# Odd rows of u reversed in DRAM and loaded apart, in a linear-attention and S4 kernel whose order is a written list

## The chip, the cores and the metric

The kernel runs on one core of one Trainium2 chip. The metric is the device time of one execution in microseconds (us). The kernel before takes 230.46 us, the median of three runs (230.1, 230.46 and 230.79).

The core has five engines with a queue of instructions each: TensorE (PE in the profile; its weight loads are shown as PEld), VectorE (DVE), ScalarE (ACT), GpSimd (POOL) and SyncE (SP). Here SP only starts DMA transfers; ACT starts some, too. A queue is worked off in order: an instruction that waits holds up what stands behind it.

## The reference

Two independent halves are computed and put side by side in the output (2048 rows, 448 + 448 columns).

```python
# half A: linear attention with a softmax feature map (16 heads of 28)
qkv = (x @ wqkv)...
pq = einsum("bhsd,hdf->bhsf", q, w_phi);  pk = einsum("bhsd,hdf->bhsf", k, w_phi)
phi = concatenate([softmax(p), softmax(-p)])      # for q and for k
kv = einsum("bhsf,bhsd->bhfd", phi_k, v);  z = einsum("bhsf->bhf", phi_k)
a = (phi_q @ kv) / (phi_q . z + 1e-6), heads joined, @ wo
# half B: S4 convolution, D = 448 channels, N = 256 states, L = 2048
P = exp(dt * A * l)                               # complex, l = 0 .. L-1
K = einsum("dn,dnl,dn->dl", C, P, dt * B).real
y = irfft2(rfft2(K padded) * rfft2(u padded))[:L] + u * Dskip
return concatenate([a, y])
```

The change touches half B: how u comes in, and how one table of powers is made.

## The kernel before, in words

**Order.** The program doesn't issue an instruction when its line is reached. Each line adds an operation to a list (`Prog.add`), in program order, and at the end `prog.run(ORDER)` issues them in the order of a list of numbers written into the source. `ORDER` thus sets the order on every engine's queue. Three more lists go with it: `PLACES` gives each buffer its byte offset in one large SBUF tile (`sb`), so that buffers share bytes when their uses lie apart, `SLOTS` gives each PSUM product its banks, and `PICKS` says for each copy whether ACT or DVE makes it ("A", "V") and for each DMA whether SP or ACT starts it ("S", "Q"). The framework adds the waits: for data, and for bytes or banks that an earlier operation still uses.

**Half B.** The convolution goes through a transform of length 1024 for each of two blocks of u. `signal_spectrum(b)` makes u's spectrum. It needs, for each block, the even rows of u and the odd rows in reverse order, their sum `ab[:, 0]` and their difference `ab[:, 1]`; then 16 groups of products with the cosine tables `G1[0]` and `G1[1]` (512 KB each), whose results go to DRAM (`SUd`). Before, `load_u` brings pairs of rows (an even and the next odd row, 1792 bytes together) with two transfers of 64 partitions a block, and the odd rows are turned round on PE: four products with an anti-identity matrix, `REV`, and two copies out of PSUM to a buffer `ur`.

The kernel K is made from powers of exp(dt A). For the exponents 128, 16, 8, 32 and 64, ACT makes an exponential, a cosine and a sine, and DVE multiplies them (`PW`, each product 128 x 1792). The 256th powers come from squaring the 128th: `s2` are squares, `q256` takes the real part (`sub`) and the imaginary part (`stt`) in f32, and a copy writes it to `PW[256]` as bf16 with the two halves of each group of 56 columns interleaved. `TM`, `CB` are products of the coefficients with the 8th powers. Then, four times for a quarter of the channels (`tables(qt)`), DVE builds tables `U_` and `W` of powers, PE multiplies them (`build_k`), the result passes through DRAM (`scatter_k`) and PE transforms it (`kernel_spectrum`). `conv(qt)` multiplies the spectra on DVE and transforms back on PE (`inverse`).

**Half A** (`key_side`, `query_side`) is interleaved with this by `ORDER`.

**Line numbers.** Helpers record most operations: L186 is any DVE tensor-tensor operation (`tt`), L198 the DVE operation with a scalar and two tensors (`stt`), L206 an ACT function (`af`), L214 a copy, L217 a scaled copy, L229 PE products (`mms`), L239 PE transposes, L245 a transposing DMA, L249 a plain DMA.

Of the kernel before, what the change touches and what calls it, by code (L numbers as in the profile page):

```python
# [9 lines left out]
BF16 = mybir.dt.bfloat16  # L10
# [41 lines left out]
def _dft_tables():  # L52
# [24 lines left out]
    pid = np.zeros((128, 6, 128))  # L77
    for i, p in enumerate(ODD + [-1]):
        pid[np.arange(128), i, np.arange(128)] = p
    pid[np.arange(128), 5, 127 - np.arange(128)] = 1.0  # L80
# [49 lines left out]
def kernel(  # L130
# [22 lines left out]
    SUd = dram.tile([4, 128, 8, D_MODEL], BF16, name="SUd")  # L153
    KTd = dram.tile([4, 3, 128, D_MODEL], BF16, name="KTd")
# [36 lines left out]
    def add(o, a, b):  # L191
        tt(o, a, b, ALU.add)

    def sub(o, a, b):
        tt(o, a, b, ALU.subtract)
# [51 lines left out]
    def dma(eng, o, i):  # L247
        e = {"S": nc.sync, "Q": nc.scalar}[prog.queue()]
        prog.add("S", lambda: e.dma_start(out=o, in_=i))  # L249

    PID = sb([128, 6, 128])
# [3 lines left out]
    REV = PID[:, 5, :]  # L255
# [16 lines left out]
    def row_pairs(row, a):  # L272
        rs = u2.ap[0][0]
        return bass.AP(tensor=u2.tensor, offset=u2[row + 128 * (1 - a), 0].offset,
                       ap=[[2 * rs, 64], [256 * rs, 4], [1, 2 * D_MODEL]])

    ua = [sb([128, 4, 2, D_MODEL]) for _ in range(2)]

    def load_u(b):
        for a in range(2):  # L280
            dma("S", ua[b][64 * a:64 * a + 64].rearrange("p t r d -> p t (r d)"), row_pairs(1024 * b, a))

    eye = sb([112, 112])
# [75 lines left out]
    q128, q256 = (sb([128, 2, NCOL], F32) for _ in range(2))  # L359
# [24 lines left out]
    sub(q256[:, 0, :], s2[:, 0, :], s2[:, 1, :])  # L384
    stt(q256[:, 1, :], q128[:, 0, :], -2.0, q128[:, 1, :], ALU.mult, ALU.mult)
    copy(view(PW[256][:, 0, 0:1], [56, 32], [1, 2], [2, 28]), view(q256[:, 0, 0:1], [56, 32], [28, 2], [1, 28]))
# [32 lines left out]
    def signal_spectrum(b):  # L419
        ab = sb([128, 2, 4, D_MODEL])  # L420
        ur = sb([128, 4, D_MODEL])
        for tp in range(2):
            bs = prog.banks(2)
            mms([(psum[:, bs[k], 0:D_MODEL], REV, ua[b][:, 3 - 2 * tp - k, 1, :], dict(start=True, stop=True))
                 for k in range(2)])
            copy(ur[:, 2 * tp:2 * tp + 2, :], two(bs))
        add(ab[:, 0], ua[b][:, :, 0, :], ur)
        sub(ab[:, 1], ua[b][:, :, 0, :], ur)
# [459 lines left out]
).split()]  # L888
PLACES = [64 * int(i) for i in (
# [52 lines left out]
```

## Time and profile before

| | us |
|---|---|
| median of three runs | 230.46 |
| the profiled execution | 230.0 |
| its span, first to last instruction | 228.1 |
| DVE busy | 211.7 |
| PE busy | 201.5 |
| ACT busy | 194.5 |
| POOL busy | 8.9 |

The span's 40 slices are 5.7 us each; the digits in them are tenths of a slice. A "form" is an operation with its shapes. In a group of instructions "busy" is the time covered and the mean is that of one instruction, from its start to its end; neighbours on an engine overlap by some 0.1 us, so a run of them takes a little less than their sum. For DMAs, KB is the size of one transfer, and the time is from issue to landing. [...]

### The profile page before, as it was taken

What the parts mean: (1) busy time and instruction counts of PE and PEld (TensorE: products, weight loads), DVE (VectorE), ACT (ScalarE), POOL (GpSimd) and SP (SyncE); (2) the same over time, 40 slices, a digit from 0 to 9 for tenths busy, and PEclk for the clock granted to TensorE, in tenths of its full rate; (3) what the DMA queues carried; (4) which work ended last, traced back from release to release, by engine and by line L of the source; (5) the groups of instructions that cost most, each with busy time, mean ns of one, the idle gap of its engine ahead of it and who ended that gap; (6) DMA issues with size and microseconds to landing.
All of it is one profiled execution on the core that took longest, in us unless ns stands there. A gap on an engine that the chain in (4) does not pass through costs nothing.

```text
span 228.1 us, 7325 instructions
## 1 busy us (share of the span) xinstructions
PE 201.5 (88%) x3136; PEld 145.8 (64%) x3136; DVE 211.7 (93%) x268; ACT 194.5 (85%) x354; POOL 8.9 (4%) x26
## 2 busy tenths in 40 slices
PE   1155699999999999999795999999999998999994
PEld 1053346555558555897573878645677875799994
DVE  1899999999999999999999999999999994999990
ACT  3999999999999999999999999999798866454431
POOL 4000000200000200020000000100000000000000
PEclk9999889999999999999999999999999999999999
DMA  5969911548569959987757426053999149664163
GB/s 158 231 150 271 284 29 35 119 165 210 134 161 161 189 101 251 99 218 188 238 77 199 85 67 203 3 68 56 263 288 178 23 101 177 94 122 75 40 168 80
DMA packets 78247, 32.87 MB, mean 144 GB/s; under 512 B 64856, under 2 KB 76168, under 8 KB 77960
## 3 DMA queue, kind: packets, MB, share of 16 engines
q1 hardware_dynamic: 73080, 29.99, 60.8%
q10 hardware_dynamic: 5136, 2.43, 4.1%
q8 instruction: 24, 0.39, 0.7%
q14 instruction: 7, 0.06, 0.1%
HBM read 15.84 MB, written 8.49 MB: 107 GB/s over the span
## 4 chain that ended last, share of the span: by engine, by line
PE 53%; ACT 23%; DVE 16%; issue 5%; DMA 1%; DVEq 0%; ACTq 0%
PE psum L229 52%; DVE sbuf L186 14%; ACT sbuf L206 13%; ACT sbuf L214 9%; DVE sbuf L214 2%; DMA sbuf<-in_B_log_dt_dram 1%; ACT L206 1%; PE psum L239 1%; DVE sbuf L217 1%; DVE sbuf L198 0%; DVEq L186 0%; ACTq L206 0%; DVEq L214 0%; DVE sbuf L309 0%
## 5 line engine op out<-in xcount | busy, mean ns | idle before, releaser
L229 PE MATMUL psum<-sbuf 128*128 128x112 bf16 (+10 forms) x3088 | 199.3, 257 | 22.6 <-ACT sbuf L214 8.8
L186 DVE TENSOR_TENSOR sbuf<-sbuf 128x896 bf16<-128x896 bf16 (+11 forms) x214 | 190.6, 946 | 5.8 <-ACT sbuf L206 4.3
L229 PEld LDWEIGHTS <-sbuf 128*128 128x128 bf16 (+5 forms) x3088 | 143.3, 112 | 77.4 <-issue 23.9
L214 ACT CAST sbuf<-psum 128x448 bf16<-128x448 f32 (+8 forms) x124 | 80.1, 700 | 21.7 <-PE psum L229 19.0
L206 ACT ACTIVATE sbuf<-psum 128x512 bf16<-128x512 f32 (+6 forms) x154 | 83.5, 631 | 1.8 <-PE psum L229 1.0
L206 ACT ACTIVATE sbuf<-sbuf 128x896 bf16<-128x896 bf16 (+3 forms) x29 | 18.9, 684 | 2.4 <-DMA sbuf<-in_B_log_dt_dram 1.2
L214 DVE CAST sbuf<-psum 128x448 bf16<-128x448 f32 (+4 forms) x21 | 12.2, 596 | 7.0 <-PE psum L229 6.5
L206 ACT ACTIVATE sbuf<-psum,sbuf 128x896 f32<-128x896 f32 (+3 forms) x17 | 14.0, 827 | 0.5 <-ACT sbuf L214 0.5
L224 POOL MEMSET sbuf<- 128x224 bf16 (+7 forms) x21 | 8.4, 429 | 152.3 <-PE psum L229 67.3
L214 ACT COPY sbuf<-psum 112x896 bf16<-112x896 bf16 (+2 forms) x12 | 7.2, 638 | 2.1 <-PE psum L239 1.9
L203 ACT ACT_TABLE_LOAD x5 | 6.4, 1283 | 1.3 <-PEq L926 1.3
L206 ACT ACT_TABLE_LOAD x4 | 5.1, 1283 | 0.1
L214 DVE COPY sbuf<-sbuf 128x448 bf16<-128x448 bf16 (+2 forms) x13 | 4.2, 327 | 0.0
L239 PE MATMUL psum<-sbuf 112*112 112x112 bf16 (+1 forms) x48 | 3.4, 216 | 0.9 <-DVE sbuf L186 0.9
L239 PEld LDWEIGHTS <-sbuf 112*112 112x112 bf16 (+1 forms) x48 | 2.9, 120 | 1.5 <-DVE sbuf L186 1.0
L186 DVE TENSOR_TENSOR sbuf<-psum,sbuf 128x448 bf16<-128x448 f32 (+1 forms) x6 | 2.8, 489 | 0.0
L214 DVE CAST sbuf<-sbuf 128x1792 bf16<-128x1792 f32 (+1 forms) x4 | 2.8, 688 | 0.0
L217 DVE TENSOR_SCALAR sbuf<-sbuf 128x1568 bf16<-128x1568 bf16 x4 | 2.5, 617 | 0.0
L214 ACT COPY sbuf<-sbuf 128x224 bf16<-128x224 bf16 (+1 forms) x5 | 2.2, 444 | 0.0
L220 ACT ACTIVATE sbuf<-sbuf 128x1792 f32<-128x1792 f32 x1 | 1.8, 1785 | 0.0
L217 ACT ACTIVATE sbuf<-sbuf 112x448 bf16<-112x448 bf16 x1 | 0.6, 576 | 0.8 <-DVE sbuf L309 0.8
L198 DVE SCALAR_TENSOR_TENSOR sbuf<-sbuf,psum 128x128 f32<-128x128 f32 x4 | 1.1, 282 | 0.0
(8 smaller groups left out, 2.5 us busy)
## 6 DMA issues: line engine op xcount, KB each, us to landing
SUd<-sbuf SPq DMA_DIRECT2D x8, 448.0 KB, 3.6
sbuf<-SUd SPq DMA_DIRECT2D x4, 896.0 KB, 5.0
sbuf<-const SPq DMA_DIRECT2D x8, 384.0 KB, 4.2
sbuf<-in_B_u_dram SPq DMA_DIRECT2D x4, 448.0 KB, 6.3
out_dram<-sbuf SPq DMA_DIRECT2D x13, 112.0 KB, 2.8
out_dram<-sbuf SPq DMA_DIRECT2D x3, 448.0 KB, 3.5
sbuf<-const SPq DMA_DIRECT2D x2, 512.0 KB
sbuf<-const ACTq DMA_DIRECT2D x1, 1024.0 KB
```

The lines of the kernel that those rows point to most:

```text
L186: prog.add("V", lambda: nc.vector.tensor_tensor(out=o, in0=a, in1=b, op=op))
L198: prog.add("V", lambda: nc.vector.scalar_tensor_tensor(out=o, in0=a, scalar=s, in1=b, op0=op0, op1=op1))
L203: nc.scalar.preload_act_table_set("natural_log_exp_and_others")
L206: nc.scalar.activation(o, a, fn, **kw)
L214: either(lambda: nc.scalar.copy(o, a), lambda: nc.vector.tensor_copy(o, a))
L217: either(lambda: nc.scalar.activation(o, a, ACT.Copy, scale=s), lambda: nc.vector.tensor_scalar_mul(o, a, s))
L220: either(lambda: nc.scalar.activation(o, a, ACT.Square), lambda: nc.vector.tensor_tensor(out=o, in0=a, in1=a, op=ALU.mult))
L224: prog.add("G", lambda: nc.gpsimd.memset(o, v))
L229: nc.tensor.matmul(o, lhsT=l, rhs=r, **kw)
L239: nc.tensor.transpose(o, i, idn)
```

## The change

The source is changed in three places, and the four lists are written anew.

1. u. `reverse_u(b)` copies the odd rows of a block, last row first, from u in DRAM to a new DRAM tile `URd[b]` (4 x 128 rows of 896 bytes, 448 KB). `load_u(b)` then loads the even rows into `ua[b][0]` and the reversed odd rows into `ua[b][1]`, in one transfer of 448 KB each. The anti-identity matrix, its eight products, the four copies and the buffers `ur` go. Since even rows no longer lie in swapped halves of the partitions, the table G's rows are permuted.
2. `PW[256]`. The f32 buffer `q256` goes. The subtraction writes bf16 to `PW[256]` directly, in the interleaved order, and the imaginary part does so in two operations of 448 columns, one per half. The copy goes.
3. `ORDER`, `PLACES`, `SLOTS`, `PICKS`. There are 1042 operations in place of 1048. In the new numbering 0 and 1 are the two reversals, 2 loads log_dt, 5 and 7 to 11 load A_re, A_im, C_re, B_re, C_im and B_im, 28 loads the key weights, 34 to 37 load w_phi, 39 and 40 load G1[0] and G1[1], 41 to 44 load u (even rows, reversed rows; block 0, block 1), and 12 to 27 are the transposing loads of x. On SP's queue this gives the order: log_dt, A_im, C_im, B_im, B_re, a w_phi piece, C_re, **reversal 0**, even rows 0, G1[1], **reversed rows 0**, even rows 1, key weights, **reversal 1**, an x load, G1[0], a w_phi piece, an x load, **reversed rows 1**, and then the other loads of x and the weights.

On DVE the new list begins: PW8, PW64 and PW16 products, `ab0-` (block 0's difference), PW128, `TM`, `ab0+`, one half of PW256's imaginary part, CB (imaginary), PW256's real part, CB (real), PW32, a small `U_` product, the other half of PW256's imaginary part, `ab1+`. Before, it was PW8, 16, 64, 128, 32, `TM`, a small copy, `ab0-`, `ab0+`, CB twice, the imaginary part of q256, a small copy, `ab1+`, `ab1-`.

```diff
-    pid = np.zeros((128, 6, 128))
+    pid = np.zeros((128, 5, 128))
...
-    pid[np.arange(128), 5, 127 - np.arange(128)] = 1.0
+    G = G[np.arange(128) ^ 64]
...
+    URd = dram.tile([2, 4, 128, D_MODEL], BF16, name="SRd")
...
-    ua = [sb([128, 4, 2, D_MODEL]) for _ in range(2)]
+    ua = [[sb([128, 4, D_MODEL]) for _ in range(2)] for _ in range(2)]
+
+    def u_rows(row, *dims):
+        return bass.AP(tensor=u2.tensor, offset=u2[row, 0].offset, ap=[[n * u2.ap[0][0], m] for n, m in dims] + [[1, D_MODEL]])
+
+    def reverse_u(b):
+        dma("S", URd[b], u_rows(1024 * b + 255, (256, 4), (-2, 128)))
 
     def load_u(b):
-        for a in range(2):
-            dma("S", ua[b][64 * a:64 * a + 64].rearrange("p t r d -> p t (r d)"), row_pairs(1024 * b, a))
-
+        dma("S", ua[b][0], u_rows(1024 * b, (2, 128), (256, 4)))
+        rev = URd[b, 3, 0:1]
+        dma("S", ua[b][1], bass.AP(tensor=rev.tensor, offset=rev.offset,
+                                   ap=[[D_MODEL, 128], [-128 * D_MODEL, 4], [1, D_MODEL]]))
+
+    for b in range(2):
+        reverse_u(b)
...
-    sub(q256[:, 0, :], s2[:, 0, :], s2[:, 1, :])
-    stt(q256[:, 1, :], q128[:, 0, :], -2.0, q128[:, 1, :], ALU.mult, ALU.mult)
-    copy(view(PW[256][:, 0, 0:1], [56, 32], [1, 2], [2, 28]), view(q256[:, 0, 0:1], [56, 32], [28, 2], [1, 28]))
+
+    def pairs_in(t):
+        return view(t[:, 0:1], [56, 16], [28, 2], [1, 28])
+
+    def pairs_out(t):
+        return view(t[:, 0:1], [56, 16], [1, 2], [2, 28])
+    sub(pairs_out(PW[256][:, 0, :]), pairs_in(s2[:, 0, :]), pairs_in(s2[:, 1, :]))
+    for e in range(2):
+        re_, im_ = (view(q128[:, i, 28 * e:28 * e + 1], [56, 16], [1, 28]) for i in range(2))
+        stt(view(PW[256][:, 1, e:e + 1], [56, 16], [2, 28]), re_, -2.0, im_, ALU.mult, ALU.mult)
...
-        ur = sb([128, 4, D_MODEL])
-        for tp in range(2):
-            bs = prog.banks(2)
-            mms([(psum[:, bs[k], 0:D_MODEL], REV, ua[b][:, 3 - 2 * tp - k, 1, :], dict(start=True, stop=True))
-                 for k in range(2)])
-            copy(ur[:, 2 * tp:2 * tp + 2, :], two(bs))
-        add(ab[:, 0], ua[b][:, :, 0, :], ur)
-        sub(ab[:, 1], ua[b][:, :, 0, :], ur)
+        add(ab[:, 0], ua[b][0], ua[b][1])
+        sub(ab[:, 1], ua[b][0], ua[b][1])
...
 ORDER = [int(i) for i in (
-    "1 69 0 3 2 43 28 44 46 5 45 7 8 36 47 62 51 64 52 54 55 53 60 6 61 9 59 30 63 56 40 49 39 79 48 58 67 57 80 50 "
+    "206 38 30 751 2 5 7 10 11 9 45 6 3 4 46 48 47 49 53 56 33 37 63 8 0 41 65 54 57 59 66 55 64 40 62 81 42 61 50 "
+    "82 43 28 87 88 51 1 52 60 79 58 67 83 78 89 23 80 74 109 174 176 178 75 68 39 36 69 76 179 70 94 180 175 26 108 "
+    "44 92 177 96 90 120 13 122 91 85 84 121 29 20 95 123 181 86 198 208 183 201 124 93 139 199 404 203 204 115 182 "
...
 PICKS = (
-    "SSSSSSSSSSSSSSSSSSSSAAVVVAAAVAVAAAAAAAAASAASAASAASAAAAAAAAASAASAASAASSSSSSSSSVVVVVAAAASSSSSSSSAAAAAA"
+    "SSQSSSSSSSSSSSSSSSSSSSAAVVVAAAVAAAAAAAASAASAASAASAAAAAAASAASAASAASSSSSSSSSAVAVAAAAASSSSSSSSAAAAAAAAA"
...
```

More of the change, by code (lines that the diff above doesn't have):

```diff
@@ L249, in dma @@
         prog.add("S", lambda: e.dma_start(out=o, in_=i))
-    PID = sb([128, 6, 128])
+    PID = sb([128, 5, 128])
     ident = PID[:, 0, :]
@@ L254 @@
     NEG = PID[:, 4, :]
-    REV = PID[:, 5, :]
     bias_hp = sb([128, 1], F32)
@@ L270, in load_x @@
             dma_t(xT[:, j, 512 * i:512 * i + 512], x2, 512 * i, 1, 512, XCOL[j])
[L272 to L275, printed above, removed]
-    ua = [sb([128, 4, 2, D_MODEL]) for _ in range(2)]
-    def load_u(b):
-        for a in range(2):
-            dma("S", ua[b][64 * a:64 * a + 64].rearrange("p t r d -> p t (r d)"), row_pairs(1024 * b, a))
+    ua = [[sb([128, 4, D_MODEL]) for _ in range(2)] for _ in range(2)]
[3 more added lines that the diff above has]
+        dma("S", URd[b], u_rows(1024 * b + 255, (256, 4), (-2, 128)))
+    def load_u(b):
+        dma("S", ua[b][0], u_rows(1024 * b, (2, 128), (256, 4)))
[4 more added lines that the diff above has]
+        reverse_u(b)
     eye = sb([112, 112])
@@ L358 @@
     cs = {k: sb([128, 2, NCOL], F32) for k in LOWP}
-    q128, q256 = (sb([128, 2, NCOL], F32) for _ in range(2))
+    q128 = sb([128, 2, NCOL], F32)
     CR = sb([128, 2, NCOL])
@@ L849 @@
 ORDER = [int(i) for i in (
[38 rows of a table removed]
[37 rows of a table added]
 ).split()]
 PLACES = [64 * int(i) for i in (
[12 rows of a table removed]
[12 rows of a table added]
 ).split()]
 SLOTS = [[int(c) for c in i] for i in (
[5 rows of a table removed]
[4 rows of a table added]
 ).split()]
 PICKS = (
-    "SSSSSSSSSSSSSSSSSSSSAAVVVAAAVAVAAAAAAAAASAASAASAASAAAAAAAAASAASAASAASSSSSSSSSVVVVVAAAASSSSSSSSAAAAAA"
-    "AAAAAAAAAAAVVVSSSSVVVAVAAAASSSSSSSSSSSSSSSSAVAAAAVAASVVAAAAAASQAVAAAAAVASSASASAAASAQVVVAVVAAASQSSSSS"
-    "SAAAVAAVAAAAAAAAAVQSASASAAASASVVAAAVVVVSQSSSQQSAVAAAAAAAAAAAAAAASSVSASASASAVAAAAAASVSASAQVSAQAQ"
+    "SSQSSSSSSSSSSSSSSSSSSSAAVVVAAAVAAAAAAAASAASAASAASAAAAAAASAASAASAASSSSSSSSSAVAVAAAAASSSSSSSSAAAAAAAAA"
+    "AAAAAAAAAVASSSSVVAVVAAAASSSSSSSSSSSSSSSSAVAAAVAVASVVAAAAAASSAAAAAAAVASSAQASAAASASVVVVAVAAASSSSSSSSAA"
+    "AAAAAVVAAAAAAVVSSASASAAASASVVAAVAVAASQSSQSQSAAAAAAAAAAAAVAAVAQSAQASAQASAAAAAAVASASVQVQVSAQVS"
 )
```

104 rows, old and new, of tables (ORDER, PLACES, SLOTS) are left out of this document.

## The prediction

> **What bounds the kernel now.** I read the page first, its busy shares and slices; then the windows, to see which engine is full where; then the chain of waits for the end; then DVE's timeline around u; last the DMA views, since the change makes two new transfers. The page:
>
> ```profile
> span 228.1 us, 7325 instructions
> ...
> PE 201.5 (88%) x3136; PEld 145.8 (64%) x3136; DVE 211.7 (93%) x268; ACT 194.5 (85%) x354; POOL 8.9 (4%) x26
> ...
> PE   1155699999999999999795999999999998999994
> ...
> DVE  1899999999999999999999999999999994999990
> ACT  3999999999999999999999999999798866454431
> ...
> DMA  5969911548569959987757426053999149664163
> GB/s 158 231 150 271 284 29 35 119 165 210 134 161 161 189 101 251 99 218 188 238 77 199 85 67 203 3 68 56 263 288 178 23 101 177 94 122 75 40 168 80
> ```
>
> Three engines are nearly full at once, and PE is idle mainly in the first five slices (to 28.5 us). The windows, whose columns are the stretch, the busy time of each engine with its instructions, the granted clock and the DMA's share and rate, sharpen it:
>
> ```profile
> 20.00:30.00 10.00, 7.95 (x32) 4.10 (x31) 10.00 (x11) 9.97 (x16) 0.00 (x0) 0.83 1.03 267
> ...
> 10.00:183.70 173.70, 159.92 (x2264) 108.87 (x2265) 172.33 (x217) 168.37 (x306) 6.31 (x14) 0.99 0.67 150
> ...
> 194.40:225.00 30.60, 30.50 (x568) 28.80 (x567) 27.74 (x30) 12.90 (x26) 0.00 (x0) 1.00 0.52 104
> ```
>
> DVE is busy 172.33 of the 173.70 us that end with the last `W` table of quarter 3; then PE works 30.50 of the last 30.60. The chain of waits names the same two at its ends:
>
> ```profile
> 15.40 2.03 DVE sbuf L186
> ...
> 171.96 13.73 PE psum L229 x290
> ...
> 194.37 30.54 PE psum L229 x568
> ```
>
> So a microsecond taken from DVE before 183.7 should come off the end, and a microsecond in which DVE waits there is added; PE work saved before 28.5 us is worth nothing by itself.
>
> **The change part by part.** DVE's timeline at the place (start, length, operation, count) and the forms' rows (busy, mean ns):
>
> ```profile
> 13.46 11.70 DVE L186 TENSOR_TENSOR sbuf<-sbuf 128x1792 bf16<-128x1792 f32 x6 [0.19 <-ACT sbuf L206]
> 25.26 3.16 DVE L186 TENSOR_TENSOR sbuf<-sbuf 128x1792 bf16<-128x1792 bf16 x4
> L198 DVE SCALAR_TENSOR_TENSOR sbuf<-sbuf 128x896 f32<-128x896 f32 x1 | 1.1, 1084 | 0.0
> L198 DVE SCALAR_TENSOR_TENSOR sbuf<-sbuf,psum 128x128 f32<-128x128 f32 x4 | 1.1, 282 | 0.0
> L186 DVE TENSOR_TENSOR sbuf<-sbuf 128x896 f32<-128x896 f32 x1 | 1.1, 1083 | 0.0
> L214 DVE CAST sbuf<-sbuf 128x1792 bf16<-128x1792 f32 x2 | 2.3, 1128 | 0.0
> L214 ACT CAST sbuf<-psum 128x896 bf16<-128x896 f32 x27 | 25.4, 997 | 0.0
> L229 PE MATMUL psum<-sbuf 128*128 128x448 bf16 x392 | 81.8, 360 | 4.9 <-ACT sbuf L214 4.8
> L214 DVE CAST sbuf<-psum 128x448 bf16<-128x448 f32 x14 | 8.6, 623 | 2.0 <-PE psum L229 1.6 <-ACT sbuf L206 0.4
> L214 DVE COPY sbuf<-sbuf 128x448 bf16<-128x448 bf16 x7 | 2.8, 401 | 0.0
> ```
>
> *The powers.* Gone are 1.08 + 1.08 + 1.13 = 3.29 us of DVE. In their place come the subtraction, with a bf16 result in strides of two, and two operations of 448 columns. No row has that result; f32 sources kept the 896-column rows at 1.08 us whichever operation, so I take 1.08, and by the line between 282 ns for 128 and 1084 for 896 columns 0.62 each: 2.32 in all, 1.0 us saved. Were the strides to double the three, 4.6 us would stand there, 1.3 lost; nearest is the same operation without strides, so I keep the gain.
>
> *Copies that change engine.* Up to the last `W` of quarter 3 the new `PICKS` take from DVE four PSUM copies of 448 columns and give it three (-0.6 us), take three and give one of the SBUF copies (-0.8), and swap small ones, which, with four operations fewer whose ends overlap a neighbour, makes about +0.4. DVE has 2.0 us less to do before 183.7, the end of this run of the last table:
>
> ```profile
> 179.74 3.94 DVE L186 TENSOR_TENSOR sbuf<-sbuf 128x896 bf16<-128x896 bf16 x5
> ```
>
> ACT gets most of the copies, 18 operations for 14 given, but loses the four `ur` copies, 4 x 25.4/27 = 3.8 us: it gets no fuller.
>
> *PE.* Eight products of 448 columns go, 8 x 0.21 = 1.7 us, all before 28.5 us, where PE waits for others: nothing. The permuted G is another constant: nothing. `ab` is added from contiguous halves, the same form: nothing.
>
> *Queues.* The load of the identities moves to ACT's queue, between the first exponential and a scaled copy; about 0.43 us to issue, covered by the 0.77 us that ACT idles there. Without that cover it would cost ACT those 0.4 us, not the end. Some output stores change queue with their data; nothing follows them but other stores.
>
> ```profile
> 4.75 0.58 ACT L217 ACTIVATE sbuf<-sbuf 112x448 bf16<-112x448 bf16 x1 [0.77 <-DVE sbuf L309]
> 0.80 0.43 ACTq L289 DMA_DIRECT2D sbuf<-in_B_A_re_dram  x1
> ```
>
> *The reversals.* This is the open price: the trace has no copy from DRAM to DRAM. On SP, `load_u`'s reversed rows must wait for the copy's landing, and SP holds behind that wait, for block 0, even rows 1, the key weights and reversal 1, and for block 1 all other loads of x and Wq. DVE waits for the reversed rows at `ab0-` and `ab1+`. When does it want them? `ab0-` follows three products: 13.46 + 3 x 1.95 = 19.3 us. `ab1+` follows all six of that run (11.70), `ab0` and CB (3.1), the new powers (2.2 with overlap) and a small product (0.3): 30.8 us.
>
> When do they come? It hangs on how many of the 16 engines carry the copy. The DMA rows:
>
> ```profile
> DMA packets 42, 0.05 MB, mean 67 GB/s; under 512 B 14, under 2 KB 42, under 8 KB 42
> ...
> q10 hardware_dynamic: 272, 0.06, 13.1%
> ...
> SUd<-sbuf SPq DMA_DIRECT2D x8, 448.0 KB, 3.6
> sbuf<-in_B_u_dram SPq DMA_DIRECT2D x4, 448.0 KB, 6.3
> sbuf<-in_B_A_im_dram SPq DMA_DIRECT2D x1, 224.0 KB
> out_dram<-sbuf SPq DMA_DIRECT2D x1, 56.0 KB, 1.6
> ```
>
> The first is the window 108.3 to 109.1, in which one 28-row load of `KV` goes: 28 data packets and 14 small ones. The second is ACT's last store, 128 rows in two runs: 256 and 16. So a transfer ends with one small packet per engine, and 28 outer rows used 14 engines, the largest divisor up to 16, where 128 used 16. The reversal's outermost count is 4 (256 u rows apart): by this it runs on four engines, 112 KB each, and whatever SP issues after it queues behind that on these four.
>
> [...]
>
> On sixteen engines the six raw loads (224 KB each) are through at 5.7 + (1.376 - 0.90)/0.231 = 7.8 us, by the first two slices' rates. On each of the four engines then come, in SP's order: reversal 112 KB, u 28, G1[1] 32, reversed rows 28, u 28, key weights 24.5, reversal 112, x 8, G1[0] 32, x 8, reversed rows 28: 441 KB, 451 thousand bytes. One engine's rate: 267/16 = 16.7 GB/s in the full window 20 to 30, 288/16 = 18.0 in the best slice, and 392 KB more in 2.0 us more from the 56 KB to the 448 KB store, 12.5. With 1 us from last byte to landing (the 1.6 us of the small store less issue), block 1's reversed rows land at 7.8 + 451/18.0 + 1 = 33.9 us, at 35.8, or at 44.9: 3.1, 5.0 or 14.1 us after DVE wants them. The nearest rows are the two full stretches; I take the middle, 4.0. `ab0-` is late by 0.9 to 1.8 us on the same reckoning, within those. G1[0], on the same four engines, lands at about 33 and holds PE's fifth `signal_spectrum` group and, behind it, ACT's folds, for less than that.
>
> *The sum*, against the profiled execution's own 230.0 us (span 228.1 and 1.9 around it): 230.0 - 2.0 + 4.0 = 232.0. The median of the runs is 0.46 above it: 232.5.
>
> **The rivals.**
>
> *The copy is hidden* (the other side). If it spread over 16 engines, all 4.6 MB up to reversal 1 would be through at 7.8 + 3.2/0.267 = 19.8, the reversed rows of block 1 would follow at some 25.5, and DVE would never wait: 230.46 - 2.0 = 228.5. The same comes of four engines at 451/(30.8 - 8.8) = 20.5 GB/s each or more; at 18.8 wait and saving cancel. For it: the GB/s row's rates are of busy stretches, and four engines alone may do better. Against it: 18.0 is the best in any slice, and a count of 14 for 28 rows. [...]
>
> *The four engines hold SP as well.* If a full queue on them delays SP's later issues, or they write DRAM at 12.5 GB/s, DVE waits 8 to 14 us: 237 to 242. For it: the store row; against it: that row's fixed part is in its slope.
>
> *The new lists slip.* Copy hidden, but DVE or ACT waits elsewhere: the old list leaves DVE 1.4 us idle in 173.7, so a reordering has much to spoil; four new holes of 0.5 us eat the gain: 230.5.
>
> *The powers don't gain*, doubled strides: +2.3 against the forecast, 234.8; it would show as 4.6 us in three operations.
>
> **How the numbers follow.** Forecast, four engines and a wait of 2.8 to 7 us: 0.52. Hidden: 0.30. SP held: 0.08. Lists slip: 0.10. The powers are within these. A measurement tells 0.3% (0.7 us) from no change. Faster comes from hidden, 0.30; same from slipping lists, 0.08; slower from the rest, 0.62. Predicted 232.5; the forecast's own range is 231.2 to 235.5, and with the hidden case and part of the slow tail 228.2 to 237.0.
>
> **What would show it.** Two DVE waits for DMA or SP before `ab0-` and `ab1+`, the second ending near 35 us; SP idle ahead of the reversed-row loads; reversal landings of 8 us or more, with a low DMA share meanwhile; three `PW256` operations of 1.1, 0.6 and 0.6 us; the last `W` operation 2 us later than 183.7; a PE tail of the same 30.5 us. The prediction is wrong if reversal 1 lands before 27 us, or if DVE is full from 13 us on and yet the end moves.

## The result and the profile after

The changed kernel takes 229.39 us, the median of 20 runs (227.89 to 230.95); the kernel before, on the same chips, 230.88 (20 runs, 229.53 to 233.7). The ratio is 0.9937, with a 95% interval of 0.9908 to 0.9966: faster by 0.6%. Forecast was 232.5, slower; in its number, what happened (0.9937 x 230.46 = 229.0) is nearest to the rival in which the copy is hidden, 228.5. Ratios here and below leave out disturbed runs, those more than 1.5% above their kernel's fastest, so a ratio can differ from that of two medians.

The profiled execution took 229.43 us, its span is 227.7. The page's first lines and DVE's slices (tenths of 5.7 us each):

```profile
span 227.7 us, 7295 instructions
...
PE 201.0 (88%) x3120; PEld 145.0 (64%) x3128; DVE 210.5 (92%) x264; ACT 192.6 (85%) x354; POOL 8.1 (4%) x26
...
DVE  1799999999999999999899799999999999997992
```

The busy shares are those of before to a per cent. New are holes in DVE's row: 8 in the slice from 108 us, 7 in the one from 125 and in the one from 205. The windows (stretch; busy time of PE, PEld, DVE, ACT, POOL with their instructions; granted clock; share of the 16 DMA engines; GB/s):

```profile
20.00:30.00 10.00, 9.18 (x37) 4.49 (x38) 10.00 (x10) 9.98 (x14) 0.00 (x0) 0.67 1.03 188
19.50:20.50 1.00, 0.00 (x0) 0.00 (x0) 1.00 (x2) 1.00 (x3) 0.00 (x0) 0.65 0.27 92
...
60.00:110.00 50.00, 47.63 (x864) 33.89 (x864) 48.38 (x60) 49.40 (x109) 4.26 (x9) 1.00 0.79 171
10.00:183.70 173.70, 158.69 (x2241) 107.67 (x2250) 169.54 (x211) 166.48 (x305) 6.07 (x15) 0.97 0.69 160
...
10.00:184.72 174.72, 159.68 (x2248) 108.01 (x2256) 170.56 (x213) 167.35 (x308) 6.07 (x15) 0.97 0.69 161
```

The last table ends at 184.72 us now (shown below), so it is the last row that compares with the 172.33 of 173.70 before. Up to the end of the last table DVE works 170.56 us, 1.8 less, close to the 2.0 of the prediction. But it idles 4.16 us there, against 1.37: 2.8 more, and so the table ends 1.0 us later. The second row is the reversing copy by itself: between 19.5 and 20.5 us hardly anything else is under way, 0.27 of 16 engines, that is 4.3, are busy, and they move 92 GB/s. So the copy does run on four engines, at 21 (92/4.3) to 23 (92/4) GB/s each. Whether that is above the prediction's 16.7 to 18.0 because few engines are at work or because of the kind of transfer isn't shown.

DVE's timeline where the prediction put its two waits, and the end of the last table (three stretches; start, length, operation, count, and idle time before it in brackets, where there is any):

```profile
19.37 3.02 DVE L187 TENSOR_TENSOR sbuf<-sbuf 128x1792 bf16<-128x1792 bf16 x2
...
25.25 0.66 DVE L199 SCALAR_TENSOR_TENSOR sbuf<-sbuf 128x448 bf16<-128x448 f32 x1
25.80 4.42 DVE L187 TENSOR_TENSOR sbuf<-sbuf 128x896 bf16<-128x896 bf16 x5
30.14 0.66 DVE L199 SCALAR_TENSOR_TENSOR sbuf<-sbuf 128x448 bf16<-128x448 f32 x1
30.69 1.07 DVE L187 TENSOR_TENSOR sbuf<-sbuf 128x1792 bf16<-128x1792 bf16 x1
...
180.78 3.94 DVE L187 TENSOR_TENSOR sbuf<-sbuf 128x896 bf16<-128x896 bf16 x5
```

No bracket stands in the first five rows: block 0's difference starts at 19.37 us, where the prediction had DVE want it at 19.3, and block 1's sum at 30.69 behind its neighbour, for 30.8, and their data are there. The last table ends at 180.78 + 3.94 = 184.72, not at 181.7 (2 us ahead of 183.7), but 1.0 later than before.

SP's queue (L250 is a plain DMA, L246 a transposing one; the length is the time until SP can go on):

```profile
4.78 0.78 SPq L250 DMA_DIRECT2D SRd<-in_B_u_dram  x1
5.60 3.05 SPq L250 DMA_DIRECT2D sbuf<-in_B_u_dram  x1
8.70 1.21 SPq L250 DMA_DIRECT2D sbuf<-const  x1
13.81 0.36 SPq L250 DMA_DIRECT2D sbuf<-SRd  x1
...
15.32 0.64 SPq L250 DMA_DIRECT2D SRd<-in_B_u_dram  x1
16.01 5.15 SPq L246 DMA_TRANSPOSE sbuf<-in_A_x_dram  x1
...
25.79 0.52 SPq L250 DMA_DIRECT2D sbuf<-SRd  x1
```

SP waits 3.9 us (9.91 to 13.81) for reversal 0 to land, 9.0 us after its issue. The issue right behind each reversal takes 3.05 and 5.15 us, and a second x load 3.39, in place of about 0.5 and 1.3: SP is held, as a rival said, though two issues between the x loads take 0.52 and 0.41. The reversed rows of block 1 are issued at 25.79 with no wait for reversal 1, so that had landed by then.

The rows were in time, but not by much. The chain of waits shows block 0's, and that of a second profiled execution (`after_again`, below) block 1's; the last row is DVE's timeline in that one:

```profile
4.78 9.02 DMA SRd<-in_B_u_dram
13.81 3.51 DMA sbuf<-SRd
...
26.14 3.98 DMA sbuf<-SRd
...
30.58 1.08 DVE L187 TENSOR_TENSOR sbuf<-sbuf 128x1792 bf16<-128x1792 bf16 x1
```

Block 0's rows landed at 13.81 + 3.51 = 17.32 us, 2 us before its difference starts; block 1's at 30.12, 0.5 us before its sum.

The last step of the chain of waits is 194.21 to 224.66, 30.45 us of PE, as before (194.37, 30.54).

### The profile page after: what moved, and what is told of

It reads as the page before. It is cut to its first block, busy times and chain, and to the rows that moved or that the text cites. A ratio compares the mean times of both kernels' runs of the same rounds, so it can differ in the third digit from the quotient of the medians.

```text
span 227.7 us, 7295 instructions
## 1 busy us (share of the span) xinstructions
PE 201.0 (88%) x3120; PEld 145.0 (64%) x3128; DVE 210.5 (92%) x264; ACT 192.6 (85%) x354; POOL 8.1 (4%) x26
## 4 chain that ended last, share of the span: by engine, by line
PE 48%; DVE 26%; ACT 12%; DMA 7%; issue 5%; SPq 0%; DVEq 0%
PE psum L230 48%; DVE sbuf L187 24%; ACT sbuf L215 8%; DMA SRd<-in_B_u_dram 4%; ACT sbuf L207 4%; DMA sbuf<-in_B_A_re_dram 2%; DMA sbuf<-SRd 2%; DVE sbuf L215 1%; DVE sbuf L199 1%; ACT L204 1%; DVE sbuf L218 0%; PE psum L240 0%; SPq L250 0%; DVEq L215 0%; DVEq L187 0%
## 5 line engine op out<-in xcount | busy, mean ns | idle before, releaser
L230 PE MATMUL psum<-sbuf 128*128 128x112 bf16 (+9 forms) x3072 | 199.0, 256 | 22.9 <-DVE sbuf L187 11.9
L187 DVE TENSOR_TENSOR sbuf<-sbuf 128x896 bf16<-128x896 bf16 (+10 forms) x214 | 191.2, 948 | 7.3 <-ACT sbuf L207 3.6
L215 ACT CAST sbuf<-psum 128x448 bf16<-128x448 f32 (+7 forms) x120 | 76.1, 699 | 20.4 <-PE psum L230 11.9
L207 ACT ACTIVATE sbuf<-psum 128x512 bf16<-128x512 f32 (+5 forms) x154 | 84.2, 635 | 4.9 <-PE psum L230 3.4
L215 DVE CAST sbuf<-psum 128x448 bf16<-128x448 f32 (+5 forms) x21 | 12.7, 608 | 4.2 <-PE psum L230 3.3
L215 ACT COPY sbuf<-sbuf 128x224 bf16<-128x224 bf16 (+2 forms) x9 | 4.2, 494 | 0.0
L215 DVE COPY sbuf<-sbuf 128x448 bf16<-128x448 bf16 (+1 forms) x9 | 2.8, 310 | 0.6 <-PE psum L230 0.5
L215 DVE CAST sbuf<-sbuf 128x1792 bf16<-128x1792 f32 (+1 forms) x2 | 1.3, 660 | 0.0
L199 DVE SCALAR_TENSOR_TENSOR sbuf<-sbuf 128x448 bf16<-128x448 f32 x2 | 1.3, 658 | 0.0
```

Of the source, the lines that this page charges most:

```text
L187: prog.add("V", lambda: nc.vector.tensor_tensor(out=o, in0=a, in1=b, op=op))
L199: prog.add("V", lambda: nc.vector.scalar_tensor_tensor(out=o, in0=a, scalar=s, in1=b, op0=op0, op1=op1))
L207: nc.scalar.activation(o, a, fn, **kw)
L215: either(lambda: nc.scalar.copy(o, a), lambda: nc.vector.tensor_copy(o, a))
L230: nc.tensor.matmul(o, lhsT=l, rhs=r, **kw)
```

## The experiments

"Changed kernel" is the one after; "stand" is idle time of PE that the profile puts down to "issue", which is nothing that it shows.

### Was the copy hidden, and what if it weren't?

The changed kernel once more; then its copies on sixteen engines:

```diff
-        dma("S", URd[b], u_rows(1024 * b + 255, (256, 4), (-2, 128)))
+        dma("S", URd[b].rearrange("t (h i) d -> (t h) i d", h=4), u_rows(1024 * b + 63, (64, 16), (-2, 32)))
...
+            for h in range(4):     # reversed rows: four loads of 32 partitions
```

and then cut into four pieces of every row, with the outermost count of 4 as before:

```diff
-        dma("S", URd[b], u_rows(1024 * b + 255, (256, 4), (-2, 128)))
+            for c in range(4):
+                e.dma_start(out=URd[b][:, :, 112 * c:112 * c + 112], in_=...)   # 224 bytes of each row
```

> The changed kernel once more, beside the three edits below on the same chip. Theory A (the reversing copy is hidden: its four DMA engines ran at about 22.9 GB/s each, not the 16.7 to 18.0 of the prediction, so VectorE never waits for it, and VectorE's smaller work is the gain): ratio to before 0.991 to 0.997. Theory B (the copy is hidden from VectorE but still costs time through SyncE, which stood 5.15 us at one transposing load and 3.39 us at another): the same ratio here; the two part in the next run.

> The changed kernel with both reversing copies written with an outermost count of 64 in place of 4, so that they spread over all 16 engines, and the reversed rows loaded by four transfers of 32 partitions. Theory A: VectorE did not wait for the copy before, so the time is that of the changed kernel within 0.5 us (about 229.4). Theory B: SyncE is no longer held behind four full engines, so the transposing loads and the second half of the signal's table come 3 to 5 us earlier, and the time falls by 1 us or more (228.4 or less).

> The changed kernel with each reversing copy cut into four transfers of 224-byte pieces of the rows, four times the packets on the same four engines, so that the copies are late. Theory A (the copy is hidden because it was quick enough, and VectorE would pay for any lateness): VectorE now waits ahead of block 0's difference and block 1's sum, the latter for 4 to 10 us in place of none, and the time rises by as much as these waits, 233 to 241. Rival E (the order has slack there, so that a late block 1 is absorbed): under 231.

Measured: 0.9961 (0.9916 to 1.0006) for the changed kernel, 0.9950 (0.9915 to 0.9986) with sixteen engines, 1.0430 (1.0367 to 1.0492) with pieces. SP's queue with sixteen engines:

```profile
10.68 1.74 SPq L287 DMA_DIRECT2D sbuf<-SRd  x4
...
14.11 1.32 SPq L246 DMA_TRANSPOSE sbuf<-in_A_x_dram  x1
...
19.83 1.74 SPq L287 DMA_DIRECT2D sbuf<-SRd  x4
```

That these are sixteen engines is the author's reading of the outermost count of 64; measured is a DMA share of 1.02 in 10 to 20 us, 0.80 in the changed kernel. The reversed rows are issued 3 and 6 us earlier and the x load holds SP 1.32 us in place of 5.15, yet the two ratios differ by 0.1%. So on four engines the copy costs DVE nothing, and through SP nothing that these runs can tell; with intervals of some 0.4%, up to about 1 us isn't excluded. With pieces, DVE's waits (us in total, times, longest):

```profile
DVE sbuf L187 <- DMA sbuf<-SRd: 8.7, 2, 6.1
```

The span is 239.0, 11.3 above the changed kernel's, for 8.7 us of these waits. So the mechanism of the forecast exists: where the rows are late DVE waits, and the end moves. Only the copy wasn't late. What made the other 2.6 us isn't separated; PE also waited 8.2 us for a load of constants.

### Each part alone, with the old lists

The two parts were put into the kernel before one at a time and together, its own lists kept as far as they go. First with block 1's sum about 5 us further back in the order, so that its rows can land, the u part alone and both parts:

> The reversal by copy alone, with the old lists as in the run above and the old 256th powers. No VectorE operation is taken away by this part alone: the copies that TensorE's reversal needed were ScalarE's. Theory A (only VectorE's work moves the end): as before, 230.4 to 231.4. Rival D (TensorE's eight products and ScalarE's four copies gone, so the signal's spectrum starts earlier, is the gain): 229.9 or less. If the copy is late: VectorE waits ahead of block 1's sum and the time is up by that wait.

> Both parts of the change (reversal by copy, 256th powers in place) with the four lists of the kernel before: order, places, slots and picks are the old ones, but for the operations that are gone or new, and block 1's sum and difference stand about 2 us later so that its reversed rows can land. Theory A with idle VectorE as the new lists' price (VectorE idled 4.16 us in 10 to 183.7 us against 1.37 before, so they gave back 1 us or more of the gain): 228.0 to 229.6, not slower than the changed kernel. Rival C (the new lists are the gain; the change alone brings little, for it takes only 1.0 us from VectorE when no copy changes its engine): 229.6 to 230.4, slower than the changed kernel. Were the old order ill matched (a wait for the reversed rows before block 1's sum), 231 or more, and that wait is in the trace.

(In the second of these, half of the 256th powers are overwritten in their place before they are used, so a part of the computation is changed.) Measured: 1.0276 (1.0223 to 1.0329) and 1.0300 (1.0258 to 1.0341). The window of the first says why; DVE worked 29.99 us there before:

```profile
30.00:60.00 30.00, 25.68 (x165) 14.26 (x164) 23.90 (x36) 21.43 (x29) 0.52 (x1) 0.87 0.40 91
```

PE waited for block 1, ACT for PE (6.3 us ahead of one copy), and DVE for ACT. A sum a few us late by order alone costs 6.5 us.

With block 1's sum in its old place (SP's order, in words):

```diff
 SP: ... Bim, +reversal 0, WV, even rows 0, +reversal 1, identities, even rows 1, x load, reversed rows 0,
     G1[1], two x loads, Wq, a w_phi piece, reversed rows 1, G1[0], ...   (the other engines as before)
```

> The reversal by copy alone, as in the run of the u part before this one, where block 1's sum had been moved about 5 us back in the order and the time rose by 6.5 us; here it keeps its old place in VectorE's order, and the loads of that stretch stand ahead of it in SyncE's. VectorE's own work is as before. Theory A: as before within 0.5 us (230.4 to 231.4) if the reversed rows land by 29.5 us, where block 1's sum stood; each microsecond that they land later costs one to one and a half. Rival D (TensorE's and ScalarE's work taken away is the gain): 229.9 or less.

> Both parts with the old lists, block 1's sum in its old place. Theory A with the new lists as a price: 229.4 to 230.2, that is the sum of the two single runs and no slower than the changed kernel. Rival C (the new lists bring the gain): slower than the changed kernel by 0.5 us or more, 230.2 to 231.

> The kernel before with the 256th powers alone changed (subtract and two halves straight into the bf16 table, no f32 buffer, no casting copy; the three stand together where the copy's neighbours stood, since the table's place holds other data until then); order, places, slots and picks else the old ones. VectorE has 1.0 us less to do before 183.7 us (3.29 against 2.32 us). Theory A (VectorE's work is the bound and a microsecond there is a microsecond at the end): 0.5 to 1.0 us faster than before, 229.9 to 230.4. Rival C (what is saved early is given back at VectorE's later waits for TensorE and ScalarE): same as before within 0.3 us.

> The 256th powers alone with the old lists once more, now at their old places in VectorE's order (in the run before this one of the kind they stood together 4 us later, and ScalarE's exponentials waited 1.37 us for the place of the squares that they read); the damping buffer of the first quarter is put elsewhere so that the table's place is free. VectorE has 1.0 us less to do. Prediction's step: 1.0 us faster, 229.9. Rival H: within 0.4 us of before, with new VectorE waits of 0.6 us or more.

| with the old lists | ratio to before (95%) |
|---|---|
| u part alone | 1.0052 (1.0015 to 1.0089) |
| both parts | 1.0059 (1.0025 to 1.0092) |
| powers alone, three together | 1.0051 (1.0020 to 1.0082) |
| powers alone, old places | 1.0009 (0.9987 to 1.0032) |

No part is faster by itself, and both together aren't either. The powers at their old places, 1.0 us less of DVE, leave the time as it was. Rival C, that the change brings nothing without new lists, has the direction, but its number was too low: 230.2 to 231 for both parts, where 1.0059 is 231.8. The u part alone, 231.7, is also above the 230.4 to 231.4 that were expected. The kernels with the u part have eight TensorE products fewer than the kernel before, so their later matmuls lie elsewhere among PE's instructions; 60 matmuls added to the kernel before moved its time by 1.1%, as shown further down.

### Does a microsecond of DVE reach the end?

First less work in the kernel before (a part of the powers' table is left out), then more, in both kernels, each time in the operations of the 256th powers:

```diff
-    sub(q256[:, 0, :], s2[:, 0, :], s2[:, 1, :])
+    sub(q256[:, 0, 0:448], s2[:, 0, 0:448], s2[:, 1, 0:448])    # the product likewise, the copy 448 columns of 1792
```

```diff
-    sub(q256[:, 0, :], s2[:, 0, :], s2[:, 1, :])
+    prog.add("V", re256)      # the same subtract three times; in the changed kernel that of PW[256]
```

> The kernel before with the three VectorE operations of the 256th powers cut short: subtract and multiply on half of their columns, the casting copy on a quarter, the rest of the table left with what lay there (a part of the computation is left out). VectorE has about 1.8 us less to do at 28 to 41 us, and no list, place or engine is touched. The prediction's step (a microsecond taken from VectorE before 183.7 us comes off the end): 1.8 us faster, 229.1. Rival H (VectorE's lead ends in waits for ScalarE and TensorE, which are as full as VectorE in 60 to 110 us, 49.88 and 48.87 of 50): 230.4 to 230.9, with new VectorE waits that sum to 1.3 us or more.

> The kernel before with the subtract of the 256th powers carried out three times in place of once (36.1 us, 1.09 us each): VectorE has 2.1 us more to do there, and all else is as it was. Prediction's step (VectorE full, a microsecond there is a microsecond at the end): 2.1 us slower, about 232.9, ratio 1.009. Rival H with room in both directions: less than 0.8 us slower.

> The changed kernel with the same subtract three times (26.3 us, 1.16 us each): 2.3 us more for VectorE, which gives back the whole of what the change took from it. Prediction's step: 2.3 us slower than the changed kernel, 231.7 to 232.5. Rival H (VectorE's lead is spent in waits of 1.6 to 2.6 us behind 60 us anyway): 229.5 to 230.8, with fewer VectorE waits there.

Measured: 1.8 us less, 1.0016 (0.9992 to 1.0040); 2.1 us more in the kernel before, 1.0055 (1.0027 to 1.0082), that is 1.3 us; 2.3 us more in the changed kernel, 1.0095 (1.0060 to 1.0130) against its own 0.9937 and 0.9961, 3.1 to 3.7 us, each give or take about 1. It isn't symmetric: more DVE work is paid for, less is not rewarded. Where the 1.8 us went is in the timeline of the cut kernel, two rows of it, and in its window:

```profile
33.62 0.62 DVE L217 TENSOR_SCALAR sbuf<-sbuf 128x1568 bf16<-128x1568 bf16 x1 [0.46 <-ACT sbuf L206]
...
51.57 1.93 DVE L186 TENSOR_TENSOR sbuf<-sbuf 128x896 bf16<-128x896 bf16 x3 [0.79 <-ACT sbuf L206]
```

```profile
30.00:60.00 30.00, 29.59 (x207) 16.98 (x206) 28.75 (x44) 29.90 (x44) 0.52 (x1) 1.00 0.49 124
```

By 52 us DVE has waited 1.25 us for ACT, and ACT is busy 29.90 of these 30 us. It was just as full in the kernel before, with PE close behind:

```profile
30.00:60.00 30.00, 29.65 (x208) 17.15 (x207) 29.99 (x44) 29.90 (x44) 1.38 (x1) 1.00 0.45 124
60.00:110.00 50.00, 48.87 (x854) 34.15 (x852) 49.85 (x64) 49.88 (x108) 3.63 (x7) 1.00 0.81 160
```

So three engines set the pace together; this is read from the windows and the waits, for no run takes work from ACT or PE. Two misses: in the kernel before 2.1 us more cost 1.3, not 2.1, and in the changed kernel 2.3 us cost at least that, where rival H had expected less. Of the seven runs behind this last number four had a granted clock of 0.970 or 0.971 and took 233.56 to 234.31 us; the three at 0.993 took 231.89, 231.96 and 233.47. A part of it may be the clock's.

### The stands of PE

One idle piece of the kernel before lies on the path to its end and has no releaser. PE's timeline from the last table to the tail, before:

```profile
185.91 6.05 PE L229 MATMUL psum<-sbuf 128*128 128x448 bf16 x143
192.98 1.12 PE L229 MATMUL psum<-sbuf 128*32 128x80 bf16 x49 [1.03 <-issue]
194.37 30.52 PE L229 MATMUL psum<-sbuf 128*128 128x112 bf16 x568 [0.27 <-DVE sbuf L214]
```

and after:

```profile
186.88 7.16 PE L230 MATMUL psum<-sbuf 128*128 128x448 bf16 x192
194.21 30.44 PE L230 MATMUL psum<-sbuf 128*128 128x112 bf16 x568 [0.17 <-ACT sbuf L215]
```

The same 192 products, with a stand of 1.03 us in them before and none after. So from the end of the last table to the tail it is 10.69 us before (183.68 to 194.37) and 9.49 after (184.72 to 194.21): all that the profiled execution gained (228.1 to 227.7), and more. In five of the six kernels with the old lists whose timeline was read there the stand comes back in the same run of products (0.37 to 1.00 us). In the DMA views a queue of its own, q8 (kind "instruction"), moves 24 packets of 0.39/24 MB = 16 KB. That they are PE's instructions is read from their pace: 3136 products, with as many weight loads, to 24 packets are 131 each, and between the packets that start at 198.6, 206.3, 212.5 and 219.4 us, in the tail, PE makes 135, 127 and 134 (elsewhere the counts spread more, 42 to 231). In the kernel before one of these packets starts in the window 190.5 to 190.6; none does in 189 to 190.5, nor in 192 to 194.4:

```profile
q8 instruction: 1, 0.02, 75.9%
```

PE goes on at 192.98, 2.4 us after that start. The author's reading, Theory F below, is that PE had run through the instructions of one packet before the next had come. If so, matmuls added far ahead of it must move the stand:

```diff
-        items = []
+        items = [(psum[0:16, bs[0], 0:1], DG[:, 0, 0:16], DG[:, 0, 0:1], dict(start=True, stop=True))] * pad
```

One column each, in a stretch ahead of 13.5 us in which PE idles over 5 us, before the products of the coefficients. Nothing else is touched.

> The kernel before with 60 matmuls of one column added in TensorE's idle stretch between 6.4 and 12.1 us, so that every later matmul lies 60 places further on in TensorE's list of instructions; nothing else is changed. Theory F (TensorE's instructions come in 16 KB blocks by their own queue, and TensorE stands when it has run through one before the next has come: it stood 1.03 us at 191.95 to 192.98 us, 2.44 us after the block's packet began at 190.54, in the products of the last table that end before the tail): the stand moves to another matmul or goes; where it goes, the tail starts up to 1.0 us sooner after the last table operation (9.5 to 9.7 us after in place of 10.69) and the time falls by up to 1.0 us, 229.9 to 230.9. Theory G (the stand belongs to that matmul, a wait that the profile does not show): the stand stays where it is, 617 matmuls before the last one, and the time is as before.

> The changed kernel with 100 such matmuls between 6.5 and 13.5 us. In its profile a block's packet began when 580 matmuls were left and none when some 680 were, where the kernel before had one; 100 more ahead move that block's edge to 680 left, where the kernel before stood. Theory F: TensorE now stands 0.5 to 1.1 us inside the products of the last table, the tail starts 10.0 to 10.6 us after the last table operation in place of 9.49, and the time is up by as much, 229.9 to 230.8. Theory G: no stand there, the time as without the added matmuls (229.4 to 230.2).

> The kernel before with 30 one-column matmuls in TensorE's idle stretch ahead of 12 us. Theory F (the position against the 16 KB blocks sets one to three microseconds of stands): differs from before by 0.5 us or more, in either direction, 229.5 to 233.5, with TensorE's stands at other matmuls. Theory J (the run with 60 was slow for another reason): 230.5 to 231.2.

> The same with 100. Theory F: another place of the stands and another time, 229.5 to 233.5. Theory J: 230.5 to 231.2, or a cost that grows with the count, which would then lie ahead of 60 us.

> The changed kernel with 30. Theory F, gain of the position: within the family of the kernel before, 229.5 to 232.5. Theory K (the gain is the change's own): 229.2 to 230.2 here and with 60, lower than the kernel before at most positions.

> The changed kernel with 60. Theory F: 229.5 to 232.5, unlike the run with 30. Theory K: 229.2 to 230.2.

PE's timeline of the kernel before with 60 added, in two stretches:

```profile
71.75 2.59 PE L229 MATMUL psum<-sbuf 128*32 128x80 bf16 x124
76.08 4.19 PE L229 MATMUL psum<-sbuf 128*32 128x80 bf16 x65 [1.74 <-issue]
...
110.22 1.71 PE L229 MATMUL psum<-sbuf 128*32 128x80 bf16 x80 [1.83 <-issue]
...
190.38 7.03 PE L229 MATMUL psum<-sbuf 128*128 128x448 bf16 x192
197.65 30.54 PE L229 MATMUL psum<-sbuf 128*128 128x112 bf16 x568 [0.24 <-DVE sbuf L214]
```

The stand ahead of the tail is gone, and the tail starts 7.27 us after the first of the 192 products (190.38 to 197.65) in place of 8.46 (185.91 to 194.37), as Theory F had it. But stands of 1.74 and 1.83 us have come earlier, both 2.3 to 2.5 us after the start of a q8 packet, and both within the same kind of product, 128x80, whose matmuls follow each other by 0.02 us. At 59 us DVE is 0.02 us behind the kernel before (59.15 for 59.13), so up to there the added matmuls themselves cost nothing. PE's stands in the waits of the kernel before, of that with 60 added, and of the changed kernel with 30 added (us in total, times, longest):

```profile
PE psum L229 <- issue: 1.7, 2, 1.0
```

```profile
PE psum L229 <- issue: 4.6, 4, 1.8
```

```profile
PE psum L230 <- issue: 0.3, 1, 0.3
PE psum L240 <- issue: 0.3, 1, 0.3
```

| added | before: ratio (95%) | stands, span | changed: ratio (95%) | stands, span |
|---|---|---|---|---|
| 0 | 1 | 1.7, 228.1 | 0.9937 (0.9908 to 0.9966); 0.9961 (0.9916 to 1.0006) | 2.1, 227.7; 1.5, 227.1 |
| 30 | 0.9998 (0.9964 to 1.0032) | 3.2, 230.2 | 0.9947 (0.9897 to 0.9997) | 0.6, 225.8 |
| 60 | 1.0111 (1.0062 to 1.0159) | 4.6, 231.4 | 1.0123 (1.0073 to 1.0173) | 2.5, 230.6 |
| 100 | 0.9991 (0.9964 to 1.0019) | 2.2, 228.8 | 1.0009 (0.9978 to 1.0040) | 2.0, 232.9 (its slowest run) |

The added matmuls move the kernel before by 1.2% and the changed one by almost 2%, two to three times what the change brings. In the kernel before, the span grows with the stands, from 0 to 60 by (231.4 - 228.1)/(4.6 - 1.7) = 1.1 us for each. At 0 and 30 the changed kernel is ahead by 0.4 to 0.6%, at 60 and 100 it is behind by 0.1 to 0.2%, within the intervals. The lead at 30 is weak: the medians of all twelve runs are 231.00 and, for the kernel before with 30, 231.06. Span less stands is 226.4 to 227.0 in the four of before and 225.2 to 225.6 in three of the changed kernel; the one with 60 comes to 228.1, or to 225.5 if two of its pauses, 1.78 and 0.81 us, which the profile puts down to ACT, are taken off as well, though such pauses were not taken off the others. That with 100 is left out, as it was profiled in its slowest run. So the changed kernel may have about a microsecond of its own, which shifts as large as those of the added matmuls can hide. The intervals don't settle it. With the old lists the same difference is 229.7 - 2.6 = 227.1 for the u part and 230.3 - 2.6 = 227.7 for both parts, no less than before: if there is such a microsecond, it comes with the new lists.

Misses: with 100 added the changed kernel slowed as expected, but not by a stand inside the last table's products; with 30 and with 100 added, the time of the kernel before did not move as Theory F wanted, though with 30 its profiled execution, the slowest of its twelve, stood 3.2 us; and Theory K, the gain as the change's own, had 229.2 to 230.2 for the changed kernel at 30 and at 60, where the second gave 233.3. Stands also differ from one execution to the next: the cut kernel above has the TensorE instructions of the kernel before one for one, and stood 5.0 us in its profiled execution, the slowest of its twelve (232.99). That the scatter of the runs is made of this fits, but was not tested; nor is it shown what takes the 2.3 to 2.6 us between a packet's start and PE's going on. There is a rival for the scatter of the changed kernel: of its first 20 runs the five with a granted clock of 0.976 to 0.978 have a median of 230.63 us, the 15 at 0.984 to 1.0 one of 228.92. The kernel before was granted 0.99 or more in most of its runs. Whether the clock is the cause, no run tells; if it is, it hides a part of the changed kernel's gain.

No kernel here beats the changed one by more than its interval: its best is 0.9937, with sixteen engines 0.9950, with 30 added matmuls 0.9947.

## Why the prediction was wrong, point by point

*The reversals, "the open price".* This is the step that failed and turned the sign. That the copy runs on four engines was right (0.27 of 16 busy), though the reading behind it, one small packet per engine at a transfer's end, rests on two counts, 14 and 16 (in the window of the 28-row load the 14 start between 108.70 and 108.90 us, the last rows before 108.80). Right, too, were the landing of over 8 us, SP's idle time ahead of block 0's reversed rows and the times at which DVE wants them (19.37 and 30.69 us for 19.3 and 30.8). Mis-sized was the term of one engine's rate. The prediction took 16.7 to 18.0 GB/s from windows in which all sixteen engines were full; four alone made 21 to 23, above the 20.5 that the rival "hidden" named as its bound. With 21 to 23 the prediction's own sum, 7.8 + 451/rate + 1, gives 30.3 to 28.4 us, and 30.12 was seen. The wait was 0 in place of 4.0 us, and reversal 1 had landed before 25.79, a sign that the prediction had named for being wrong (before 27). That the rates came from busy stretches, and that four engines alone may do better, was in the prediction as an argument for the rival, and should have been given more than 0.30.

*"A microsecond taken from DVE before 183.7 us should come off the end."* This failed too, the other way. DVE had 1.8 us less to do, and the last table ended 1.0 us later, for it idled 2.8 us more. The step read 172.33 of 173.70 us as the bound and passed over ACT's 49.88 of 50 in 60 to 110 us. The cut of 1.8 us shows it by itself: no gain. With a wait of 0 and a saving worth 0 the sum would have been 230.46, no change, which is not the result either.

*The powers*: 1.16 us for the subtraction and 0.66 each, 2.48 against the 2.32 taken; no doubling. Right, and worth nothing at the end.

*Copies that change engine*: the sum with the powers was right (1.8 us less in all, for 2.0).

*PE's products, "nothing"*: nothing in the runs contradicts it; the u part alone with the old lists is no faster. What was not thought of is that eight matmuls fewer move all later ones against q8's 16 KB packets; 60 more moved the time by 1.1%.

*"The four engines hold SP as well"*: it happened, 3.05, 5.15 and 3.39 us, and cost nothing that the run with sixteen engines could tell.

*"The new lists slip"*: in part right. DVE's idle time in 10 to 183.7 us rose from 1.37 to 4.16. But without the new lists both parts gave 1.0059, so the 0.6% needs them; how much of it is a better order and how much the place of PE's instructions stays open.

*The PE tail*, 30.5 us: right. What the prediction didn't look at is the stretch between the last table and the tail, 10.69 us, in which the gain of the profiled execution lies.

## What to carry to other kernels

Before "engine X is busy 99%" becomes "a microsecond of X is a microsecond at the end", look for a second engine as full in the same windows, and price more and less separately. Take one DMA engine's rate from a stretch in which few engines run, and where only full stretches are to be had, put the bound that decides beside it. For differences under 1% in a kernel with long runs of short matmuls, compare each version at several positions of its TensorE instructions; a single pair of kernels compares their positions too. Put each run's granted clock beside its time.

## What the runs showed of the hardware that was not expected

PE stood for up to 2.4 us at a time with no releaser shown. Seven of the eight stands in the kernel before, the changed kernel and the kernel before with 60 added ended 2.3 to 2.6 us after a 16 KB instruction packet started, each in a run of 128x80 products at some 0.02 us a matmul. The author's reading is that PE had run out of instructions; no view shows that as a cause. Sixty matmuls without any work moved the stands and cost 1.1%.

Behind a copy that keeps four engines busy, three of SP's issues took 3.05, 5.15 and 3.39 us; with the same bytes under an outermost count of 64 the same three took 0.61, 1.32 and 1.32.
